# A transformer block on one Trainium2 core: one token tile loaded ahead of half a weight matrix, and two weight loads issued sooner

## The chip, the cores and the metric

The kernel runs on one core of one Trainium2 chip. The metric is the device time of one execution in microseconds (us). A set of runs is quoted by its median. The core has five engines, named as the profile names them: PE (TensorE, the matrix engine; PEld is its weight load), DVE (VectorE), ACT (ScalarE), POOL (GpSimd) and SP (SyncE). SP only issues transfers here; "SPq" is its queue.

## The reference

The reference is one block with linear attention and a gated feed-forward network (FFN), on 2048 tokens of width 1024, in bfloat16. Cut to what matters:

```python
def _A_ref(x, wqkv, wo):                      # B, S, D = 1, 2048, 1024
    H = 32; Dh = D // H
    q, k, v = ...(x @ wqkv)...                # three heads-first tensors
    phi = lambda t: jnp.where(t > 0, t + 1, jnp.exp(t)) + 1e-6
    pq, pk = phi(q), phi(k)
    kv = jnp.einsum("bhsd,bhse->bhde", pk, v)
    z = jnp.einsum("bhsd->bhd", pk)
    num = jnp.einsum("bhqd,bhde->bhqe", pq, kv)
    den = jnp.einsum("bhqd,bhd->bhq", pq, z)[..., None] + 1e-6
    return (num / den) ... @ wo

h = x + _A_ref(_layernorm(x), A_wqkv, A_wo)
h2 = h + _B_ref(_layernorm(h), W_gate, W_up, W_down)   # ((relu(gate) * up) @ W_down), F = 3584
```

## The kernel before

The tokens are cut into 16 tiles of 128. Large matrix products are done with a scheme of sums and differences of blocks that saves one block product in eight and costs DVE work: `w_sums` makes four differences of weight blocks for K (`twk`), V (`twv`) and Q (`twq`), and `x_sums` makes four sums of token blocks. Two places matter.

**The first place, the start.** Four buffers hold the incoming token tiles (`NX1 = 4`), so tile 6, the seventh, goes into the buffer of tile 2, and its load is issued by `ln1_norm(2)`, right after DVE has normalized tile 2. `load_wkv(0)` loads the first 512 columns of the K weights in two halves of 512 KB. All these calls only append to the program of each engine, in the order of the calls, so the order of the lines is the order in SP's queue and in DVE's work.

```python
def load_wkv(nt, half=None, eng="sp"):
    for hf in ([0, 1] if half is None else [half]):
        ...
        dma(sl_wkv[nt][hf], wkv[:, d0:d1, nt * NW:(nt + 1) * NW], ..., eng=eng)

def ln1_norm(st):
    ...                                   # DVE: (x - mean) * rstd
    if st in (2, 3):
        load_x1(st + NX1)                 # SP: tile 6 after tile 2, tile 7 after tile 3
```

```python
        ln1_norm(1)
        T1d(1)                            # SP: transposes of tile 1
        load_wkv(0)                       # SP: first and second half of the first K weights
        ...
        v_piece(0, 0, {5: lambda: T1c(1, 0), 7: lambda: T1c(1, 1)})
        ln1_norm(2)                       # DVE, then SP: load of tile 6
        v_piece(1, 0)
        ...
        ln1_norm(3)
        twk.pop(0)()                      # DVE: K weight difference
        ...
        ln1_stats(4)
        m5, q5 = ln1_stats_act(5)         # ACT: mean and square of tile 5
        v_piece(2, 1, {4: lambda: T1(3), 6: m5})
        q5()
        x_sums(0)
        twk.pop(0)()                      # DVE: K difference, reads the first half
        ln1_norm(4)
        T1d(4)
        m6, q6a, q6b = ln1_stats_act(6, True)
        v_piece(3, 0)
        m6()                              # ACT: mean of tile 6
        twk.pop(0)()
        ln1_norm(5)
        T1d(5)
        twk.pop(0)()                      # DVE: K difference, reads the second half
        twv.pop(0)()                      # DVE: two V differences, inputs there long before
        twv.pop(0)()
        v_piece(3, 1)
```

**The second place, the attention output products.** Step `t` of the loop does the numerators of tile `t` and the output product of an earlier tile on PE. SP's queue carries, in each step, the transposes that feed these products, a store, and in four of the steps a load of FFN weights (512 KB).

```python
        for t in range(NE, NST + LAG + 1):          # NE = 4
            if LAG <= t < NST + LAG:
                a4_mm(t - LAG)                      # PE: output product
            if t < NST:
                a2_num(t)                           # PE: numerators
                a2_div(t)                           # DVE: division; SP: transpose
            if LAG <= t < NST + LAG:
                a4_h(t - LAG)                       # DVE: residual; SP: store
                run(late_phi, 1)
            if LAG + 1 <= t < TPP + LAG + 1:
                a4_norm(t - LAG - 1)                # DVE: layer norm; SP: transpose
            if t in (5, 7, 18, 19):
                load_w_next()                       # SP: gate weights of the FFN
```

Of the kernel before, what the change touches and what calls it, by code (L numbers as in the profile page):

```python
# [132 lines left out]
def bass_sequential_preLN__linear_attn_block__glu_gated_reglu__prompt_kernel(  # L133
# [71 lines left out]
    with es:  # L205
# [148 lines left out]
        def bank(b, w=512):  # L354
            return ps[:, b, 0:w]
# [184 lines left out]
        def alloc_bank(pool, copied=False):  # L540

            b = min((b for b in pool if not (copied and b in partial)), key=lambda b: bank_last[b])
            if not copied:
                partial.discard(b)
            touch_bank(b)
            return b
# [19 lines left out]
        def dma(slot, dst_ap, src_ap, name, reads=(), writes=(), eng="sp"):  # L566
            return PL.add(eng, lambda e: e.dma_start(dst_ap, src_ap), reads=reads, writes=writes, slot=slot,  # L567
                          name=name)
# [5 lines left out]
        def load_x1(st, split=False):  # L574
            i = st % NX1
            if split:
                for c in range(NBC):
                    dma(sl_x1h[c], x1[:, i, c * BCH:(c + 1) * BCH], xv[st * P:(st + 1) * P, c * BCH:(c + 1) * BCH],
                        "ld_x1_%d_%d" % (st, c), writes=[B_x1[i][c]], eng=("sp", "act")[c])
            else:  # L580
                dma(sl_x1[i], x1[:, i, :], xv[st * P:(st + 1) * P, :], "ld_x1_%d" % st, writes=B_x1[i])
# [3 lines left out]
        def load_wkv(nt, half=None, eng="sp"):  # L585
            for hf in ([0, 1] if half is None else [half]):
                d0 = hf * WKH
                d1 = d0 + WKH
                dma(sl_wkv[nt][hf], wkv[:, d0:d1, nt * NW:(nt + 1) * NW],
                    wqkv_v[:, d0:d1, D + nt * NW:D + (nt + 1) * NW], "ld_wkv_%d_%d" % (nt, hf),  # L590
                    writes=[B_wkv[nt][hf]], eng=eng)
# [15 lines left out]
        def load_w_next():  # L607
            L = w_next[0]
            if L >= NPASS * NPAIR * 2:
                return  # L610
            w_next[0] += 1
            n_ = (L // 2) % NPAIR
            q, which = n_ - n_ % 2 + L % 2, n_ % 2
            i = L % NWG
            src = (wg_v if which == 0 else wu_v)[:, :, q * 2 * P:(q + 1) * 2 * P]
            dma(sl_w[i], wring[:, i, :, :], src, "ld_w_%d" % L, writes=[B_w[i]])
# [149 lines left out]
        def mm(out_ap, lhsT, rhs, start, stop, reads, bbuf, name, skip=False):  # L766
            return PL.add(
                "pe",
                lambda e: e.matmul(out_ap, lhsT, rhs, start=start, stop=stop, skip_group_check=skip),  # L769
                reads=reads, writes=[bbuf], name=name,  # L770
            )
# [66 lines left out]
        def ln_norm_dve(k, src_full, src_bufs, dst_ap, dst_buf, name):  # L838
            PL.add("dve", lambda e: e.tensor_scalar(out=dst_ap, in0=src_full, scalar1=mv[:, k, 0:1],
                                                    scalar2=rstd[:, k, :], op0=ALU.subtract, op1=ALU.mult),  # L840
                   reads=list(src_bufs) + [B_mv[k], B_rstd[k]], writes=[dst_buf], name=name + "_norm")
# [27 lines left out]
        def run(ops, n):  # L869
            for _ in range(min(n, len(ops))):  # L870
                ops.pop(0)()
# [19 lines left out]
        def ln1_norm(st):  # L891
            i = st % NX1
            if st in ln1_a:
                k = ln1_a[st]
                PL.add("dve", lambda e: e.tensor_scalar(out=xn[:, st % NXN, :], in0=x1[:, i, :], scalar1=s1[:, k, 0:1],
                                                        scalar2=s1[:, k, 2:3], op0=ALU.subtract, op1=ALU.mult),
                       reads=B_x1[i] + [B_s1[k][0], B_s1[k][2]], writes=[B_xn[st % NXN]], name="ln1_%d_norm" % st)
            else:
                ln_norm_dve(ln1_k.pop(st), x1[:, i, :], B_x1[i], xn[:, st % NXN, :], B_xn[st % NXN], "ln1_%d" % st)
            if st in (2, 3):  # L900
                load_x1(st + NX1)
# [24 lines left out]
        def T1c(st, hf):  # L926
            b = alloc_bank(P1_POOL)
            tb = bank_bf(b)
            for i in range(HDC):
                c = (hf * HDC + i) * P  # L930
                PL.add("pe", lambda e, i=i, c=c: e.transpose(tb[:, i, :], xn[:, 2 + st, c:c + P], ident[:]),
                       reads=[B_xc[st][hf], B_ident], writes=[B_bank[b]], name="T1c_%d" % st)
            PL.add("act", lambda e: e.activation(out=xcT[:, st, hf * HDC:(hf + 1) * HDC, :], in_=tb[:, 0:HDC, :],
                                                 func=ACTF.Identity),
                   reads=[B_bank[b]], writes=[B_xcT[st][hf]], name="evT1c_%d_%d" % (st, hf))
            partial.add(b)

        def T1d(st):
            k = st % NXN
            dma_t(sl_tx[k], xnT[:, :, st * P:(st + 1) * P], xn[:, k, :], "T1d_%d" % st, reads=[B_xn[k]],  # L940
                  writes=B_xnT[st])
            if st + NX1 < NST:
                load_x1(st + NX1)

        def xnT_buf(st, dc):
            return B_xnT[st][0 if dc < HDC else 1]
# [6 lines left out]
        def v_piece(st, h, mid=()):  # L953
            b = alloc_bank(P1_POOL)
            nt = ND2 + h
            mid = dict(mid)
            for dc in range(NDC):
                if dc in mid:
                    mid[dc]()
                if st < 2:  # L960
                    xa, bx = xcT[:, st, dc, :], B_xcT[st][dc // HDC]
                else:
                    xa, bx = xnT[:, dc, st * P:(st + 1) * P], xnT_buf(st, dc)
                mm(bank(b, NW), xa, wkv[:, dc, nt * NW:(nt + 1) * NW],
                   dc == 0, dc == NDC - 1, [bx, B_wkv[nt][0 if dc < WKH else 1]], B_bank[b],
                   "v_%d_%d" % (st, h))
            v_copy(b, st, h)
# [10 lines left out]
        def v_copy(b, st, j):  # L978
            sc, rd = (1.0, []) if st >= 2 else (rstd[:, v_k[st], :], [B_rstd[v_k[st]]])
            PL.add("act", lambda e: e.activation(out=v_out(st, j), in_=gw(bank(b)), func=ACTF.Identity, scale=sc),  # L980
                   reads=[B_bank[b]] + rd, writes=[B_v[st % NV][j]], name="v_%d_%d" % (st, j))
# [237 lines left out]
        def a2_num(st):  # L1219
            r, i, t = st // (NST // 2), (st % (NST // 2)) // 2, st % 2  # L1220
            for b_ in NB:
                touch_bank(b_)
            for g in range(NG):
                for h in range(HPG):
                    sl = slice(h * Dh, (h + 1) * Dh)
                    mm(ps[:, NB[h], g * NUW:g * NUW + Dh + 1], pqT[sl, r, t, g, i * P:(i + 1) * P],
                       kvz[sl, g, 0:Dh + 1], True, True, [B_pqT[r][t][g], B_kvz], B_bank[NB[h]],
                       "num_%d_%d" % (st, g), skip=True)
# [23 lines left out]
        def a4_mm(st):  # L1252
            k = st % NOT
            b = a4_bank[st] = min(H_PAIRS, key=lambda b: max(bank_last[b], bank_last[b + 1]))
            for nt in range(ND2):
                touch_bank(b + nt)
                for ct in range(NG):
                    mm(bank(b + nt, NW), oT[:, k, ct, :], wo[:, ct, nt * NW:(nt + 1) * NW],
                       ct == 0, ct == NG - 1, [B_oT[k], B_wo[nt]], B_bank[b + nt], "a4_%d_%d" % (st, nt))
# [704 lines left out]
            f_()  # L1964
        ln1_norm(1)
        T1d(1)
        load_wkv(0)
        for f_ in s2_[2:]:
            f_()
        twk = w_sums(wkv, bw_k, tw_k, B_TWk, "TWk", KH)  # L1970
# [2 lines left out]

        v_piece(0, 0, {5: lambda: T1c(1, 0), 7: lambda: T1c(1, 1)})
        ln1_norm(2)
        v_piece(1, 0)
        for f_ in s3:
            f_()
# [142 lines left out]
        for t in range(NE, NST + LAG + 1):  # L2121
            if LAG <= t < NST + LAG:
                a4_mm(t - LAG)
            if t < NST:
                a2_num(t)
                a2_div(t)
            if LAG <= t < NST + LAG:
                a4_h(t - LAG)
                run(late_phi, 1)
            if LAG + 1 <= t < TPP + LAG + 1:  # L2130
                a4_norm(t - LAG - 1)
            if t in (5, 7, 18, 19):
                load_w_next()
            if t >= 9:
                run(pool_t, 1)
            if 15 <= t < 19:
                s_sums()[t - 15]()
# [161 lines left out]
```

## Time and profile before

| | |
|---|---|
| three runs before the prediction | 722.75, 722.9 and 746.3 us, median 722.9 |
| the profiled execution | 723.54 us (span of the instructions 721.8 us) |
| PE's clock | 1.00 of full speed |
| PE busy | 710.7 us, 98% of the span |
| DVE busy, ACT busy | 589.0 and 358.9 us |

The run of 746.3 us is 3% above the other two. It is left out of every ratio; the median of this row still counts it (the two fast runs alone have 722.83). The second row matters later: the execution that was profiled took 0.64 us more than the median from which the prediction subtracts, and this could be seen when the prediction was made.

A line of a timeline reads: start in us, duration in us, engine, source line, operation, output and input, number of instructions. The part in square brackets is how long the engine was idle just before, and what the profile thinks ended the idling. Matmuls that follow each other are printed as one line. The bars of successive PE lines overlap a little, because matmuls are pipelined and their ends are modelled.

### The profile page before, as it was taken

How to read it: one execution, taken by the hardware profiler on the slowest of the kernel's cores; microseconds unless marked ns; L12 is line 12 of the kernel's file. 1: busy time of each engine (PE TensorE's matmuls, PEld its weight loads, DVE VectorE, ACT ScalarE, POOL GpSimd, SP SyncE). 2: the span in 40 equal slices, each digit the busy share in tenths (PEclk: the TensorE clock that was granted, in tenths of full speed). 3: DMA queues.
4: the chain of work that ended last, by engine and by line, in shares of the span. 5: the costliest groups of instructions: out<-in, count | busy, mean ns of one | idle time of the engine just before them, and what ended most of it. 6: DMA issues, size and time to landing. Idle time of an engine off the chain costs nothing.

```text
span 721.8 us, 12822 instructions
## 1 busy us (share of the span) xinstructions
PE 710.7 (98%) x4846; PEld 380.0 (53%) x4901; DVE 589.0 (82%) x1030; ACT 358.9 (50%) x626; POOL 111.4 (15%) x178
## 2 busy tenths in 40 slices
PE   8999999999999999999999999999999999999998
PEld 3344444444444444444444558865555555547887
DVE  6988867799776889889988787787889877888885
ACT  4877666764841456687756101035454445423010
POOL 3421100000360103322321002310000000000331
PEclk9999999999999999999999999999999999999999
DMA  9752244013998787999999989994555573037996
GB/s 294 260 107 71 38 128 161 12 30 67 203 231 257 237 272 238 270 314 306 294 279 268 313 251 322 311 217 116 155 159 147 156 244 90 1 92 248 323 319 186
DMA packets 195101, 144.17 MB, mean 200 GB/s; under 512 B 53984, under 2 KB 172512, under 8 KB 195040
## 3 DMA queue, kind: packets, MB, share of 16 engines
q1 hardware_dynamic: 190048, 138.77, 65.5%
q0 software_dynamic: 4032, 3.67, 3.6%
q10 hardware_dynamic: 960, 0.92, 0.4%
q8 instruction: 38, 0.62, 0.3%
q14 instruction: 23, 0.19, 0.1%
HBM read 98.76 MB, written 32.51 MB: 182 GB/s over the span
## 4 chain that ended last, share of the span: by engine, by line
PE 93%; DMA 2%; DVE 2%; issue 1%; ACT 1%; SPq 1%; ACTq 0%
PE ps L769 93%; DMA RE<-in_A_x_dram 2%; SPq L567 1%; ACT RXH L809 0%; DVE RWG L1016 0%; DVE RE L857 0%; DVE RX L1100 0%; ACT ps L774 0%; DVE RE L1674 0%; DVE RX L854 0%; DVE st L783 0%; DVE RW L991 0%; SPq L571 0%; ACT RX L850 0%; DVE RWG L1614 0%
## 5 line engine op out<-in xcount | busy, mean ns | idle before, releaser
L774 ACT ACTIVATE ps<-ps 128x512 f32<-128x512 f32 (+1 forms) x193 | 108.9, 565 | 221.7 <-PE ps L769 213.0
L769 PE MATMUL ps<-RC,RO 128*128 128x512 f16 x616 | 143.0, 369 | 0.0
L769 PE MATMUL ps<-RH,RWG 128*128 128x512 bf16 x447 | 107.9, 379 | 0.1
L769 PEld LDWEIGHTS ps<-RC,RO 128*128 128x128 f16 x616 | 60.3, 98 | 63.5
L769 PE MATMUL ps<-RC,RWG 128*128 128x512 f16 x320 | 76.9, 380 | 1.6 <-ACT ps L774 1.4
L769 PEld LDWEIGHTS ps<-RH,RWG 128*128 128x128 bf16 x448 | 43.8, 98 | 46.9
L1483 DVE TENSOR_TENSOR RAB<-ps,RAB 128x512 bf16<-128x512 f32 x56 | 37.3, 686 | 31.3 <-PE ps L769 31.3
L1683 POOL DMA_DIRECT2D out_dram<-RX x20 | 17.9, 1278 | 263.7 <-DVE RX L1674 221.5
L769 PE MATMUL ps<-RW,RE 128*128 128x512 bf16 x243 | 56.5, 379 | 1.5 <-DVE dtmp L1236 0.5
L769 PE MATMUL ps<-RH,RO 128*128 128x512 bf16 (+1 forms) x228 | 55.2, 379 | 1.5
L769 PE MATMUL ps<-RW,RAB 128*128 128x256 f16 (+3 forms) x358 | 52.5, 300 | 0.2
L769 PEld LDWEIGHTS ps<-RC,RWG 128*128 128x128 bf16 (+1 forms) x320 | 30.0, 98 | 41.5 <-ACT ps L774 7.5
L774 ACT ACTIVATE RE<-ps 128x512 f32<-128x512 f32 (+1 forms) x64 | 31.5, 503 | 37.8 <-PE ps L769 37.8
L769 PE MATMUL ps<-RAB 128*128 128x512 bf16 (+2 forms) x237 | 49.7, 348 | 0.1
L769 PEld LDWEIGHTS ps<-RW,RAB 128*128 128x128 f16 (+1 forms) x362 | 35.4, 98 | 14.4
L1674 DVE TENSOR_TENSOR RE<-ps,RE 128x512 f32<-128x512 f32 x44 | 30.2, 686 | 14.2 <-PE ps L769 13.7
L774 ACT ACTIVATE RAB<-ps 128x512 bf16<-128x512 f32 x56 | 33.3, 594 | 16.8 <-PE ps L769 16.4
L1367 DVE TENSOR_TENSOR RO<-RWG 128x1024 f16<-128x1024 bf16 x54 | 36.9, 683 | 4.5 <-DMA RWG<-in_B_W_up_dram 4.5
L769 PEld LDWEIGHTS ps<-RH,RO 128*128 128x128 f16 (+1 forms) x256 | 24.4, 98 | 29.9 <-ACT RX L774 1.5
L1478 ACT ACTIVATE RAB<-RAB 128x1024 bf16<-128x1024 bf16 x28 | 29.5, 1055 | 19.3 <-DVE RAB L1469 18.7
L769 PEld LDWEIGHTS ps<-RW,RE 128*128 128x128 bf16 x256 | 24.0, 98 | 28.7 <-DVE dtmp L1236 0.6
L1469 DVE TENSOR_TENSOR RAB<-ps,RE 128x512 bf16<-128x512 f32 x56 | 37.1, 685 | 2.2 <-PE ps L769 1.9
(170 smaller groups left out, 1169.1 us busy)
## 6 DMA issues: line engine op xcount, KB each, us to landing
RWG<-in_B_W_gate_dram SPq DMA_DIRECT2D x28, 512.0 KB, 6.3
RWG<-in_B_W_up_dram SPq DMA_DIRECT2D x28, 512.0 KB, 5.2
RW<-l_scr SPq DMA_DIRECT2D x20, 448.0 KB, 5.7
RW<-in_B_W_down_dram SPq DMA_DIRECT2D x14, 512.0 KB, 5.4
t_scr<-RW SPq DMA_DIRECT2D x14, 512.0 KB, 4.9
l_scr<-RX SPq DMA_DIRECT2D x7, 1024.0 KB, 5.9
RE<-l_scr SPq DMA_DIRECT2D x15, 448.0 KB, 4.8
RE<-in_A_x_dram SPq DMA_DIRECT2D x23, 256.0 KB, 3.6
```

The costliest lines, as they stand in the source:

```text
L567: return PL.add(eng, lambda e: e.dma_start(dst_ap, src_ap), reads=reads, writes=writes, slot=slot, name=name)
L769: lambda e: e.matmul(out_ap, lhsT, rhs, start=start, stop=stop, skip_group_check=skip),
L774: PL.add("act", lambda e: e.activation(out=dst, in_=src, func=func), reads=reads, writes=writes, name=name)
L1367: PL.add(eng, lambda e: e.tensor_tensor(out=tb(j, u), in0=f0(u), in1=f1(u), op=ALU.subtract), reads=[B_w[i + x] for x in r] + ([B_T[k + x] ...
L1469: PL.add("dve", lambda e: e.tensor_tensor(out=d, in0=src, in1=ftmp[:, u, :], op=ALU.add), reads=[bsrc, B_s5[u]], writes=[db], name=name)
L1478: PL.add("act", lambda e: e.activation(out=d, in_=d, func=ACTF.Relu), reads=[], writes=db, name=name)
L1483: PL.add("dve", lambda e: e.tensor_tensor(out=d, in0=bank(b), in1=d, op=ALU.mult), reads=[B_bank[b]], writes=[db], name=name)
L1674: PL.add(eng, lambda e: e.tensor_tensor(out=dst, in0=in0, in1=in1, op=op), reads=reads, writes=writes, name=name)
L1683: PL.add("pool", lambda e: e.dma_start(dst, src, accum_op=ALU.add), reads=[bsrc], writes=[B_hscr[st]], slot=sl, name="acc_%d_%d" % (st, dh))
```

## The change

The intent is to remove two idle spots of PE. In the start, tile 6 waits behind 1 MB of weights, so its load is put between the two halves. In the output products, a weight load stands in SP's queue right before a transpose that PE soon needs, so both loads are issued sooner.

```diff
         ln1_norm(1)
         T1d(1)
-        load_wkv(0)
+        load_wkv(0, half=0)
         for f_ in s2_[2:]:
             f_()
 ...
         v_piece(0, 0, {5: lambda: T1c(1, 0), 7: lambda: T1c(1, 1)})
         ln1_norm(2)
+        load_wkv(0, half=1)
         v_piece(1, 0)
 ...
-            if t in (5, 7, 18, 19):
+            if t in (4, 5, 18, 19):
                 load_w_next()
```

Below, "part 1" is the load order of the start and "part 2" is the earlier gate loads.

## The prediction

> **What bounds the kernel now.** I read the page's busy shares and its chain that ended last, then the chain in order of time, then the timelines of single engines around the two places that the diff touches. Busy shares and chain shares:
>
> ```profile
> PE 710.7 (98%) x4846; PEld 380.0 (53%) x4901; DVE 589.0 (82%) x1030; ACT 358.9 (50%) x626; POOL 111.4 (15%) x178
> ...
> PE 93%; DMA 2%; DVE 2%; issue 1%; ACT 1%; SPq 1%; ACTq 0%
> ```
>
> TensorE (PE) is busy 710.7 of 721.8 us. A change that takes no matmul away can win only PE's idle time, 11.1 us in the whole kernel, so nothing near 2% (14.5 us) can come of it. The question is how much of the idle time belongs to the two places. First place, the chain in order of time (start, duration, what):
>
> ```profile
> 15.80 0.43 SPq L567
> 16.27 0.51 SPq L567
> 16.89 6.53 DMA RE<-in_A_x_dram
> 23.50 1.15 ACT RXH L809 x2
> ```
>
> The first two lines are SyncE's queue issuing the two halves of the first K weights (512 KB each); the third is the load of token tile 6, the seventh (256 KB), queued behind both and landing 6.53 us later, at 23.42; the fourth is ScalarE (ACT) taking that tile's mean, which had waited. ACT, then PE, then VectorE (DVE), from their timelines (start, duration, instruction, idle before):
>
> ```profile
> 21.77 0.61 ACT L980 ACTIVATE RE<-ps 128x512 bf16<-128x512 f32 x1
> 23.50 1.06 ACT L809 ACTIVATE RXH<-RE 128x1024 bf16<-128x1024 bf16 x1 [1.12 <-DMA RE<-in_A_x_dram]
> 24.46 0.19 ACT L809 ACTIVATION_READ_ACCUMULATOR RXH<-RE 128x1 f32 x1
> 24.55 0.58 ACT L980 ACTIVATE RE<-ps 128x512 bf16<-128x512 f32 x1
> 25.03 0.59 ACT L774 ACTIVATE ps<-ps 128x512 f32<-128x512 f32 x1
> ```
> ```profile
> 23.23 1.03 PE L769 MATMUL ps<-RC,RWG 128*128 128x512 f16 x4
> 25.67 1.04 PE L769 MATMUL ps<-RC,RWG 128*128 128x512 f16 x4 [1.42 <-ACT ps L774]
> ```
> ```profile
> 26.70 1.23 DVE L991 TENSOR_TENSOR RW<-RAB,RW 128x2048 f16<-128x2048 bf16 x1
> 28.47 0.29 DVE L854 TENSOR_SCALAR RX<-RX 128x512 bf16<-128x512 bf16 x1 [0.55 <-ACT RX L850]
> 28.80 0.69 DVE L857 SCALAR_TENSOR_TENSOR RE<-ps,RX 128x512 bf16<-128x512 f32 x1
> ```
>
> ACT loses 1.12 us for the tile. Everything it does next comes late, and one of those (25.03, a copy between PSUM banks) is what PE's next product waits for: 1.42 us idle. Later DVE idles 0.55 us for an ACT exponential. From 28.47 to past 38 DVE has no marked wait: there it, and not ACT, sets the pace, and the chain runs through it up to 36.25, where PE takes over. Second place, the attention output products, SyncE and then PE:
>
> ```profile
> 183.58 0.58 SPq L567 DMA_DIRECT2D RWG<-in_B_W_gate_dram  x1
> ...
> 193.20 0.58 SPq L567 DMA_DIRECT2D RWG<-in_B_W_gate_dram  x1
> 193.89 2.54 SPq L571 DMA_TRANSPOSE RE<-RE  x1
> ...
> 198.50 1.24 SPq L571 DMA_TRANSPOSE RE<-RE  x1
> ```
> ```profile
> 198.31 0.37 PE L769 MATMUL ps<-kvz,RAB 32*128 32x33 bf16 x32
> 199.17 3.61 PE L769 MATMUL ps<-RW,RE 128*128 128x512 bf16 x16 [0.49 <-DVE dtmp L1236]
> 202.71 0.37 PE L769 MATMUL ps<-kvz,RAB 32*128 32x33 bf16 x32
> 203.44 3.40 PE L769 MATMUL ps<-RW,RE 128*128 128x512 bf16 x15 [0.35 <-DMA RE<-RE]
> ```
>
> SyncE's single queue carries the transposes that feed these products, the stores and these loads. The transpose issued at 193.89 lands 5.1 us later, at about 199.0; the one at 198.50 lands 4.6 us later, at 203.1. PE starts the products on those tiles at 199.17 and 203.44, after 0.49 and 0.35 us of idling. The first wait is put down to DVE, but that product does not read what DVE wrote; the landing at 199.0 fits it. The inputs had long been ready: DVE finished the tile moved at 193.89 at 189.2, and the one moved at 198.50 at 193.05. So the queue itself is late here.
>
> **What the Trainium skill says.** "Perfetto Trace Analysis", section "DMA Instruction — HWDGE (DVE, Sync)": the bar of such an instruction covers the taking of the descriptor generator and the generation, not the movement. The trace agrees: bars of about 0.5 us, landing 4.7 to 6.5 us after the start for the loads around 16 us; and the same kind of transpose has a bar of 1.24 us at 198.50 but 2.54 us directly behind a 512 KB load, so I count the longer bar as queueing. "DMA: Bandwidth & Descriptors", section "Queues, rings and completion order": each DMA engine takes the descriptors of one ring in ring order, though completion is not strictly first in, first out. The landings fit: tile 5 at 18.98, first half 20.5, second half 22.8, tile 6 23.4. "TensorE: Matmul & The Clock Gate", section "Back-to-back issue gap", gives about 216 ns for an isolated gap at 512 columns; here four such matmuls advance PE 0.86 to 0.87 us (26.55, 27.41, 28.27), 215 ns each, at clock 1.00. That is the pace from which I measure lost time.
>
> **Part 1, tile 6 ahead of the second half.** Nothing is added or removed; two transfers swap. Tile 6 must wait for DVE's normalization of tile 2 to release its buffer, but that ends at 11.9 us (11.36 + 0.55) and SyncE comes to it only at 16.27, so it blocks nothing. DMA moved 338 GB/s from 16 to 22 us: skipping 512 KB saves 524,288 B / 338 GB/s = 1.55 us, so the tile lands near 21.9 instead of 23.42. ACT is free at 22.38 (21.77 + 0.61): the whole wait of 1.12 us goes, with some 0.5 us to spare. The second half slips by 256 KB / 338 GB/s = 0.8 us, from 22.8 to some 23.6. Its first reader is DVE's fourth weight difference at 24.31, itself behind a DVE instruction held by POOL since 23.40; PE reads it at 26.55, or 25.45 in the new order. So it stays hidden.
>
> ACT's copy moves from 25.03 to 23.95, PE's product from 25.67 to 24.55. But this does not carry through. ACT's exponential comes 1.1 us earlier, while DVE is busy with weight differences until about 27.9 whatever ACT does. DVE gains its idle 0.55 us and no more, and from there it sets the pace until PE starts its run at 36.79. PE gives 0.55 us back at the product at 32.12, whose copy in ACT's order stands behind an exponential that waits for DVE. Both transposes of tiles 4 and 5, which DVE reads at 29.41, are issued by 24.42 and not moved; tile 4's landed in 2.7 us and by the same time tile 5's is there near 27.1. **Part 1 is worth 0.55 us.**
>
> **Part 2, gate loads two steps sooner.** The first load goes from step 5 to step 4, the second from step 7 to step 5. Step 4's place in the queue follows the store at 175.07; SyncE is idle from 175.65 to 177.66, so it is issued there for free and lands about 4.8 us later, at 180.5. The transpose at 177.66 may stretch to 2.5 us, but its product is not due before 187.0. The second load takes the place of the first, at 183.58, unchanged. At 193.20 none is left: 0.62 to 0.69 us of issue go, and the next transpose's bar should fall from 2.54 to 1.24 us, so 2.0 us in all. It lands near 193.25 + 3.1 = 196.4 instead of 199.0, and the following one, issued near 196.5 instead of 198.5, near 200. PE wants them at 198.68 and 202.5: both waits vanish. Steps without a wait are 3.865 us apart (171.25 to 198.31, seven steps); 198.31 to 206.77 took 8.46 for two. **Part 2 is worth 8.46 - 7.73 = 0.73 us**, as PE is the chain before and after. POOL's weight differences, which read the second load, run from 197.9 on in their turn behind the normalization, and lie beside PE; the later loads hang on the last output tiles and move with PE.
>
> **Sum.** 722.9 - 0.55 - 0.73 = 721.6 us, 0.18% less.
>
> **The rivals.** First, the whole 1.12 us of part 1 carries through, if DVE can be earlier after all: 721.0 us. For it: PE's largest single gap is right there. Against: DVE's weight differences stand back to back from 24.31 to 27.9. Second, the tile does not come in time, because its landing follows the slowest of the DMA engines: DMA had fallen to 86 GB/s from 22.5 to 23.0 us and to 29 in the next half, before tile 6 was reported landed. A late second half could also hold DVE at 24.31. Part 1 is then worth 0 to 0.3 us: 721.9 to 722.2. Third, in part 2 SyncE falls behind at another place: two loads in steps 4 and 5 press on the first stores and transposes and PE waits for an earlier tile, or contention elsewhere eats the gain: 722.3 to 723. Against: the transpose issued at 188.79 landed in 4.5 us, at 193.3, and was wanted at 194.75; that slack of 1.4 us is not touched, as the load ahead of it is issued at the same time as before. Fourth, the whole gain shrinks because the shift moves later transfers against each other: a few tenths either way.
>
> **Range and chances.** Both parts right gives 721.6; both rivals for the better 721.0, less 0.2 for luck; both failing 722.7. So 720.8 to 722.7 for 8 in 10. PE's idle total rules out 2% faster; 2% slower would need a new stall of 14 us or a measurement in the slow execution that one of the three runs before shows (746.3).
>
> **What would show it.** Part 1: ACT's mark of 1.12 us for the tile is gone, PE's gap before the product now at 25.67 falls from 1.42 to about 0.3 us, DVE's 0.55 us is gone, and PE's product at 37.44 starts near 36.9. Part 2: gate loads near 175.1 and 183.0 us, none near 193; no PE idle in the output products; the first FFN matmuls (228.70) start near 227.4. It is wrong if 37.44 has not moved (part 1 hidden), has moved by over 0.9 us (DVE was not the limit), if an output product waits for a transpose still, or if the 1.3 us present at 228 us are gone by the end.

## The result

| | runs in us | median |
|---|---|---|
| before, the three of above and one more | 722.75, 722.9, 723.78 (and 746.3, slow) | 723.34 |
| after | 722.08, 722.08, 722.1, 722.21 | 722.09 |

A ratio in this document is the mean time of one kernel's fast runs over the mean of the other's fast runs of the same rounds, so it is not quite the ratio of the medians quoted. Here it is 0.9986, with a 95% interval from 0.9966 to 1.0005: the same within 2%, as predicted. The 722.09 us lie in the range, 0.5 us above the point. The difference of the two medians, 1.25 us, is too large, because 723.34 counts the slow run: the three fast runs alone have a median of 722.9, and 722.09 is 0.81 us below it. The profiled execution of the changed kernel took 722.21 us.

The profile's summary page of the changed kernel, busy times and the shares of the chain that ended last:

```profile
PE 714.3 (99%) x4901; PEld 380.0 (53%) x4901; DVE 588.9 (82%) x1030; ACT 358.9 (50%) x626; POOL 110.8 (15%) x178
...
PE 95%; DVE 2%; DMA 1%; ACT 1%; issue 1%; SPq 0%; ACTq 0%
```

The loads' share of the chain has fallen from 2% to 1%, because the wait for tile 6 is out of it. The rise of PE's busy time from 710.7 to 714.3 us is no effect of the change: the count of matmuls has risen from 4846 to 4901, so 55 records were missing in the trace before. Sums of busy time are therefore no measure of gain here; start times of instructions are.

The start, ACT and then PE and then DVE of the changed kernel:

```profile
21.86 0.61 ACT L980 ACTIVATE RE<-ps 128x512 bf16<-128x512 f32 x1
22.35 1.06 ACT L809 ACTIVATE RXH<-RE 128x1024 bf16<-128x1024 bf16 x1
...
23.89 0.59 ACT L774 ACTIVATE ps<-ps 128x512 f32<-128x512 f32 x1
```
```profile
23.31 1.03 PE L769 MATMUL ps<-RC,RWG 128*128 128x512 f16 x4
24.54 1.04 PE L769 MATMUL ps<-RC,RWG 128*128 128x512 f16 x4 [0.20 <-ACT ps L774]
...
31.56 1.04 PE L769 MATMUL ps<-RW,RWG 128*128 128x512 f16 x4 [0.81 <-ACT ps L774]
...
36.88 1.03 PE L769 MATMUL ps<-RAB 128*128 128x512 bf16 x4
```
```profile
26.78 1.22 DVE L991 TENSOR_TENSOR RW<-RAB,RW 128x2048 f16<-128x2048 bf16 x1
27.92 0.28 DVE L854 TENSOR_SCALAR RX<-RX 128x512 bf16<-128x512 bf16 x1
```

ACT takes the mean of tile 6 at 22.35 without a mark of a wait (waits under 0.15 us are not marked). PE's gap has shrunk from 1.42 to 0.20 us, DVE's idle 0.55 us is gone, PE gives some of it back at 31.56 (0.81 us), and the product that began at 37.44 begins at 36.88. Each of these is what the prediction named.

The output products, SP's queue and then PE:

```profile
175.09 0.44 SPq L567 DMA_DIRECT2D RWG<-in_B_W_gate_dram  x1
...
182.98 0.59 SPq L567 DMA_DIRECT2D RWG<-in_B_W_gate_dram  x1
...
192.26 1.24 SPq L571 DMA_TRANSPOSE RE<-RE  x1
...
195.57 1.24 SPq L571 DMA_TRANSPOSE RE<-RE  x1
```
```profile
198.00 3.63 PE L769 MATMUL ps<-RW,RE 128*128 128x512 bf16 x16
...
201.87 3.63 PE L769 MATMUL ps<-RW,RE 128*128 128x512 bf16 x16
...
227.36 1.89 PE L769 MATMUL ps<-RH,RWG 128*128 128x512 bf16 x8
```

Both loads are where the prediction put them, no product waits, and the FFN begins at 227.36 (predicted 227.4). Read from this pair of traces alone, the prediction is right in every line. The experiments show that this pair was a lucky one.

### The profile page after: what moved, and what is told of

It reads as the page before. It is cut to its first block, busy times and chain, and to the rows that moved or that the text cites. A ratio compares the mean times of both kernels' runs of the same rounds, so it can differ in the third digit from the quotient of the medians.

```text
span 720.5 us, 12877 instructions
## 1 busy us (share of the span) xinstructions
PE 714.3 (99%) x4901; PEld 380.0 (53%) x4901; DVE 588.9 (82%) x1030; ACT 358.9 (50%) x626; POOL 110.8 (15%) x178
## 4 chain that ended last, share of the span: by engine, by line
PE 95%; DVE 2%; DMA 1%; ACT 1%; issue 1%; SPq 0%; ACTq 0%
PE ps L769 95%; DMA RAB<-in_A_wqkv_dram 1%; DVE RWG L1016 0%; DVE RE L857 0%; DVE RX L1100 0%; DVE RE L1674 0%; DVE RX L854 0%; DVE RH L1016 0%; ACT RXH L809 0%; DVE RC L991 0%; DVE RW L991 0%; ACT ps L774 0%; PE ps L910 0%; DVE RWG L1614 0%; SPq L567 0%
## 5 line engine op out<-in xcount | busy, mean ns | idle before, releaser
L769 PE MATMUL ps<-RH,RO 128*128 128x512 bf16 (+1 forms) x256 | 61.2, 379 | 0.0
L1367 DVE TENSOR_TENSOR RO<-RWG 128x1024 f16<-128x1024 bf16 x54 | 36.9, 684 | 4.5 <-DMA RWG<-in_B_W_up_dram 4.5
```

Source lines behind the costliest of these rows:

```text
L769: lambda e: e.matmul(out_ap, lhsT, rhs, start=start, stop=stop, skip_group_check=skip),
L1367: PL.add(eng, lambda e: e.tensor_tensor(out=tb(j, u), in0=f0(u), in1=f1(u), op=ALU.subtract), reads=[B_w[i + x] for x in r] + ([B_T[k + x] ...
```

## A measure finer than the clock

Executions of one kernel differ by more than the effect: in one set, 11 runs of the kernel before went from 722.47 to 724.91 us. The upper end has a mark: wherever a run's clock is listed, the eleven executions with a mean granted clock of 0.998 took 724.27 us or more. The only one of them that was traced (part 2 alone, below) stood 2.34 us for the very first weights, and its granted clock was 0.57 from 8 to 12 us. No edit here touches that. So the timed ratios below, with intervals of about 0.13% (0.9 us) to each side, cannot tell half a microsecond. The traces can, because starts are given to 0.01 us and the work between two fixed instructions is the same in all kernels. I use three instructions of PE, which the prediction already named: A is the product before the large gap of the start (23.23 in the trace before), B is the first product of the second group (37.44), C is the first matmul of the FFN (228.70). B and C in the trace before:

```profile
37.44 1.03 PE L769 MATMUL ps<-RAB 128*128 128x512 bf16 x4
...
228.70 1.89 PE L769 MATMUL ps<-RH,RWG 128*128 128x512 bf16 x8
```

B - A then holds what part 1 does, and C - B what part 2 does. From C to the end of the span it is 493.1 us to within 0.1 us in all traces, so nothing is given back later.

| kernel (trace) | first half of K weights lands after | A | B | C | span | B - A | C - B |
|---|---|---|---|---|---|---|---|
| before | 4.7 us | 23.23 | 37.44 | 228.70 | 721.8 | 14.21 | 191.26 |
| before, second trace | 4.1 | 22.89 | 37.19 | 227.68 | 720.8 | 14.30 | 190.49 |
| first gate load alone moved | 5.7 | 23.13 | 37.54 | 228.04 | 721.2 | 14.41 | 190.50 |
| second gate load on ACT's queue | 4.1 | 23.19 | 37.52 | 228.02 | 721.1 | 14.33 | 190.50 |
| both gate loads at step 5 | 5.7 | 23.10 | 37.40 | 230.32 | 723.4 | 14.30 | 192.92 |
| part 2 alone | 4.2 | 26.26 | 39.24 | 229.73 | 722.8 | 12.98 | 190.49 |
| before, DVE reordered | 5.9 | 23.16 | 37.56 | 228.05 | 721.2 | 14.40 | 190.49 |
| after | 4.3 | 23.31 | 36.88 | 227.36 | 720.5 | 13.57 | 190.48 |
| after, second trace | 5.8 | 23.38 | 37.36 | 227.85 | 720.9 | 13.98 | 190.49 |
| part 1 alone | 6.1 | 23.36 | 37.41 | 228.19 | 721.3 | 14.05 | 190.78 |
| after, half a difference on POOL | 4.3 | 23.50 | 37.35 | 227.85 | 721.0 | 13.85 | 190.50 |
| after, DVE reordered | 5.8 | 23.09 | 36.38 | 226.87 | 720.0 | 13.29 | 190.49 |
| part 1, DVE reordered | 5.4 | 23.33 | 37.18 | 227.72 | 720.8 | 13.85 | 190.54 |

The second column is the time from the start of the issue of the first half of the K weights to its landing. The kernel before sends exactly the same issue at this place as the kernels with part 1.

## The experiments

Ten further kernels, and the two kernels of above once more, make twelve runs in four sets; each set has its own runs of the kernel before on the same chip, and the sets ran on different chips. All gave correct outputs.

### First set: the parts alone, and the queue (median of before: 723.39 us, nine runs)

**Part 1 alone.** The theory was the prediction's: 0.55 us from part 1 and 0.73 us from part 2, independent. The edit is the first two hunks of the change, with the steps left at `(5, 7, 18, 19)`.

> Tile 6 ahead of the second half of the K weights, gate loads left at steps 5 and 7. My theory (DVE paces the chain from 28 us on): PE's idle time before the product near 24.5 us falls from 1.42 to about 0.2 us, but the product near 31.6 us idles about 0.8 us instead of 0.23, so the product at 37.44 us starts near 36.9; the waits for transposes near 199 and 203 us stay (0.49 and 0.35 us); time 0.55 us less than before. Rival (the two parts depend on each other, or the 0.55 us is lost again before the end): 0 to 0.2 us less.

Measured: 723.04 us (five runs, 722.41 to 725.08), ratio 0.9999, interval 0.9987 to 1.0012. In the trace the tile was in time, but B came at 37.41 and not at 36.9. DVE, first difference that reads the first half and later the instruction that had idled 0.55 us, and then PE:

```profile
21.73 1.23 DVE L991 TENSOR_TENSOR RC<-RAB 128x2048 f16<-128x2048 bf16 x1 [1.34 <-DMA RAB<-in_A_wqkv_dram]
...
28.45 0.29 DVE L854 TENSOR_SCALAR RX<-RX 128x512 bf16<-128x512 bf16 x1
```
```profile
32.09 1.04 PE L769 MATMUL ps<-RW,RWG 128*128 128x512 f16 x4 [1.19 <-ACT ps L774]
```

DVE stood 1.34 us for the first half of the K weights, which landed 6.1 us after its issue. Its later work shifts with it: the instruction at 28.45 no longer waits for ACT, but it starts as late as in the kernel before (28.47). PE gives back 1.19 us at 32.09 instead of 0.81. The expected waits of the transposes were also wrong: 0.15 us in all (the product at 202.71 is 4.02 us behind the one at 198.69, instead of 3.865), where the same measure gave 0.73 us in the trace before. So the part that the load order wins depends on a transfer that the change does not touch, and the second place does not always lose time with the old steps.

**Part 2 alone.** The edit is the last hunk of the change only.

> Gate loads at steps 4 and 5, start of the kernel as before. My theory: the start has the 1.42 us of PE idle time still and the product at 37.44 us does not move, no output product waits, the first FFN matmul starts near 227.97 instead of 228.70 us; time 0.73 us less than before. Rival (the queue would not have been late in the shifted kernel, or part 1 helped part 2): some of the wait for transposes stays, 0.3 us less or fewer.

Measured: 723.09 us (722.82 to 724.58), ratio 0.9996, interval 0.9983 to 1.001. No output product waits, and C - B is 190.49. The start of this one execution says nothing: PE stood for the very first weights.

```profile
8.74 2.31 PE L769 MATMUL ps<-RAB,RC 128*128 128x512 bf16 x5 [2.34 <-DMA RAB<-in_A_wqkv_dram]
```

With everything after it 2 to 3 us later, tile 6 was no longer late, and B - A is 12.98. I leave this row out of what follows on part 1.

**First gate load alone moved.** The edit:

```diff
-            if t in (5, 7, 18, 19):
+            if t in (4, 7, 18, 19):
```

> Only the first gate load moves, from step 5 to step 4; the second stays at step 7. My theory (it is the second load, directly ahead of the transpose that feeds the late product, that makes SyncE late): the waits near 199 and 203 us stay at about 0.5 and 0.3 us, time as before within 0.2 us. Rival (what counts is the total that has queued up on SyncE by then, so that the first load's place is worth as much): both waits shrink by half or more, 0.4 us less or better.

Measured: 722.96 us (722.7 to 724.68), ratio 1.0003, interval 0.999 to 1.0015. The expectation was wrong: the second load still stands in the old place (192.75), and no product waits (C - B 190.50). Either the first load was the cause, or the waits of the trace before were chance. The run has a second use. DVE in its timeline:

```profile
21.48 1.23 DVE L991 TENSOR_TENSOR RC<-RAB 128x2048 f16<-128x2048 bf16 x1 [0.92 <-DMA RAB<-in_A_wqkv_dram]
...
28.58 0.29 DVE L854 TENSOR_SCALAR RX<-RX 128x512 bf16<-128x512 bf16 x1 [0.30 <-ACT RX L850]
```

Here, in the old load order, the first half is late too (5.7 us) and DVE stands 0.92 us for it. But DVE then still waits 0.30 us for ACT, which is late because of tile 6. Two late arrivals lie side by side, and B - A is 14.41, hardly more than the 14.21 to 14.33 of traces in which the first half came early.

**Both gate loads at step 5.** This overdoes the third rival, pressure of two loads on the queue. The edit:

```diff
-            if t in (5, 7, 18, 19):
+            if t == 5:
+                load_w_next()
+                load_w_next()
+            if t in (18, 19):
                 load_w_next()
```

> Both gate loads at step 5, one behind the other; nothing at steps 4 and 7. My theory: the waits near 199 and 203 us go as in the full change, but 1 MB stands ahead of the transposes of steps 6 and 7, and the one of step 7, which had 1.4 us to spare, comes about 1.5 to 2 us later; so a new wait of 0 to 0.6 us near 194.8 us, net 0.2 to 0.7 us less than before. Rival (the first load's move to step 4 does nothing): no wait anywhere in the output products, 0.73 us less, as with steps 4 and 5.

Measured: 725.18 us (724.4 to 726.79), ratio 1.003, interval 1.0016 to 1.0043, so really longer. SP and PE:

```profile
183.51 1.21 SPq L567 DMA_DIRECT2D RWG<-in_B_W_gate_dram  x2
185.24 2.66 SPq L571 DMA_TRANSPOSE RE<-RE  x1
```
```profile
193.25 3.61 PE L769 MATMUL ps<-RW,RE 128*128 128x512 bf16 x16 [2.38 <-DMA RE<-RE]
```

The transpose directly behind the two loads (1 MB) landed 7.9 us after its start, at 193.1, where PE wanted it at 190.87. I had named a later transpose and expected 0 to 0.6 us. So loads ahead of a transpose do delay it and PE does stand for it: the mechanism behind part 2 is real. It is a question of how much slack there is in a given execution.

### Second set: is DVE now the limit, and is the queue itself the cause? (median of before: 723.1 us, eleven runs)

**Half of one weight difference on POOL, in the kernel before and in the changed one.** If DVE sets the pace after part 1, less DVE work should help after and not before. The edit to each:

```diff
+        def twv1(eng, d0, d1):
+            PL.add(eng, lambda e: e.tensor_tensor(out=TWv[:, 0, d0:d1, :], in0=wv_[:, d0:d1, NW:2 * NW],
+                                                  in1=wv_[:, d0:d1, 0:NW], op=ALU.subtract), ...)
+        twv1("pool", 0, KH // 2)
+        twv[1] = lambda: twv1("dve", KH // 2, KH)
```

> Kernel before, with half of one DVE weight difference (the second V one, 1.22 us on DVE near 25.4 us) done by POOL near 16 us: DVE's work before its exponential falls by about 0.6 us. My theory: in the kernel before ACT is late for the tile and DVE waits for it, so DVE's idle time before 28.47 us grows from 0.55 to about 1.15 us and PE's product at 37.44 us does not move; time as before within 0.2 us. Rival (DVE's work is the limit there already): 37.44 moves 0.3 to 0.6 us earlier and the time with it.

> Changed kernel with the same half of a weight difference on POOL. My theory (with the tile early, DVE is what keeps half of the won 1.12 us): DVE starts its phi work near 27.4 instead of 27.92 us, PE's idle time before the product at 31.56 us falls from 0.81 to about 0.3 us, PE's product at 36.88 starts near 36.4; 0.4 to 0.6 us less than the changed kernel, 1.7 to 1.9 less than before. Rival (PE, or the order of ACT's work, is the limit): 36.88 does not move. A third outcome: POOL's 2.3 us delay its own normalization steps and DVE waits for them; then DVE's idle time before 23.93 us grows from 0.46 us and the gain is partly lost.

Neither told the theories apart. In the kernel before, the profiled execution took 2861.66 us. PE alone was slow: it was busy 2855.8 us, while DVE was busy 603.0 us against 589.0, and yet the page shows the clock at 1.0. Its start can't be compared with the others. The other four runs were 722.71 to 722.84 (ratio 0.9992). In the changed kernel a third thing came: 722.81 us (722.65 to 722.97), ratio 0.9993, interval 0.9981 to 1.0004. POOL's new instruction and the DVE normalization that runs beside it:

```profile
15.41 2.11 POOL L1981 TENSOR_TENSOR RW<-RAB 128x1024 f16<-128x1024 bf16 x1
```
```profile
15.54 2.26 DVE L839 TENSOR_SCALAR RXH<-RE,mv,rstd 128x1024 bf16<-128x1024 bf16 x1 [0.51 <-POOL rstd L795]
```

The normalization took 2.26 us instead of 0.55 us, about until POOL was done. The Trainium skill, "SBUF — State Buffer", section "Who interferes with whom", says that DVE in certain modes and POOL need the same pair of ports, that whoever issues first gets it for its whole instruction, and that the other is fully blocked; it counts a DVE instruction of this kind among those that can. This run agrees as far as it can show: the normalization ended at 17.80, and POOL at 17.52 (ends on POOL are rough). DVE lost 1.7 us here and saved about half of a difference of 1.22 us later, so that its instruction of 27.92 began at 28.36.

**Second gate load on ACT's queue.** Step 7's load is issued by ACT instead of SP, so that SP's queue is free for the transpose.

```diff
-        def load_w_next():
+        def load_w_next(eng="sp"):
 ...
-            dma(sl_w[i], wring[:, i, :, :], src, "ld_w_%d" % L, writes=[B_w[i]])
+            dma(sl_w[i], wring[:, i, :, :], src, "ld_w_%d" % L, writes=[B_w[i]], eng=eng)
 ...
-                load_w_next()
+                load_w_next("act" if t == 7 else "sp")
```

> Kernel before, second gate load still at step 7 but issued by ACT's queue. It separates SyncE's time from the bytes. If it is SyncE's issue time and the descriptors ahead in its own ring: the transpose now at 193.89 us starts near 193.2 with a bar of about 1.24 us and both waits go, 0.7 us less than before. If it is the 512 KB on the shared DMA engines, whoever issues them: the bar stays near 2.5 us, the transpose lands about 0.6 us earlier only, and of the 0.49 and 0.35 us at least a part stays; 0.2 to 0.7 us less. The load itself costs ACT about 0.5 us, which it has to spare there.

Measured: 723.38 us (722.88 to 725.09, six runs), ratio 1.0005, interval 0.9992 to 1.0018. The output products hardly waited (C - B 190.50). It would speak for the queue, but the edit changed more than the queue: ACT issued the load at 187.94, some 5 us before SP did in the trace before (193.20). And the next run, where the unchanged kernel does not wait either, takes the rest away.

### Third set: both kernels again, and DVE's order (median of before: 722.87 us, nine runs)

**The kernel before, unchanged, as a run of its own.**

> The kernel before, unchanged, for a second trace of it: the seven experiments so far show the landing of the first half of the K weights anywhere from 4.1 to 6.1 us after its issue, and no wait for transposes near 199 and 203 us in three of the kernels that should have had it. If the profile of before was typical: the 1.12 us wait of ACT for tile 6 and both waits for transposes (0.49 and 0.35 us) are there again within 0.2 us. If the waits for transposes come from run-to-run spread of SyncE's bars: the tile wait is there, but the sum of the transpose waits is anywhere from 0 to 0.8 us. Time as before by construction; it shows the noise.

Measured: 722.54 us (722.51 to 723.14), ratio 0.9999, interval 0.9985 to 1.0012; its median is 0.33 us under that of the same kernel's other runs of the set, which shows what a difference of medians is worth here. ACT, then PE in the start:

```profile
23.25 1.06 ACT L809 ACTIVATE RXH<-RE 128x1024 bf16<-128x1024 bf16 x1 [1.21 <-DMA RE<-in_A_x_dram]
```
```profile
25.43 1.04 PE L769 MATMUL ps<-RC,RWG 128*128 128x512 f16 x4 [1.51 <-ACT ps L774]
...
37.19 1.03 PE L769 MATMUL ps<-RAB 128*128 128x512 bf16 x4
```

The wait for tile 6 is there again, so part 1 works on something that the kernel before always has. The output products, SP and PE:

```profile
192.21 0.59 SPq L567 DMA_DIRECT2D RWG<-in_B_W_gate_dram  x1
192.91 1.79 SPq L571 DMA_TRANSPOSE RE<-RE  x1
```
```profile
198.32 3.63 PE L769 MATMUL ps<-RW,RE 128*128 128x512 bf16 x16
...
202.41 3.40 PE L769 MATMUL ps<-RW,RE 128*128 128x512 bf16 x15 [0.16 <-issue]
...
227.68 1.89 PE L769 MATMUL ps<-RH,RWG 128*128 128x512 bf16 x8
```

The load stands before the transpose as it did, but the transpose has a bar of 1.79 us instead of 2.54 and landed 4.9 us after its start, at 197.8, before PE wanted it at 198.32. The product at 202.41 shows 15 matmuls instead of 16 and "issue" before it: that is a missing record and no wait, as C - B is 190.49. So the two waits of 0.49 and 0.35 us, from which the prediction worked out part 2, are not in every execution of this kernel.

**The changed kernel again.**

> The changed kernel again, for a second trace and a time beside before on the same chip. If both parts are worth what I predicted in every run: 1.2 to 1.3 us less than before. If part 1 is only worth its 0.55 us when the first half of the K weights lands early, and part 2 its 0.73 us only when SyncE is late: 0.4 to 1.0 us less on average; and in the trace the product at 36.88 us lies between 36.9 and 37.5 according to that landing (36.9 if it takes under 4.8 us from issue, 37.4 if about 6).

Measured: 722.53 us (722.68, 722.68, 721.9, 722.53, 721.83), ratio 0.9992, interval 0.998 to 1.0005. The traced one has the late first half (5.8 us), DVE idle 0.93 us for it, B at 37.36 as the second expectation said, B - A 13.98, and no wait in the output products. The timed runs look like two groups 0.8 us apart; early and late first halves would make some 0.4 us of that, and I can't show the rest.

**DVE's order changed, in the changed kernel and in the kernel before.** The theory by now: with part 1, DVE sets the pace, and a late first half costs time. Then DVE should do first what it has inputs for. A V difference, whose inputs have been there for long, goes before the K differences that need the late halves:

```diff
         x_sums(0)
-        twk.pop(0)()
         ln1_norm(4)
         T1d(4)
+        twv.pop(0)()
         m6, q6a, q6b = ln1_stats_act(6, True)
         v_piece(3, 0)
         m6()
         twk.pop(0)()
+        twk.pop(0)()
         ln1_norm(5)
         T1d(5)
         twk.pop(0)()
         twv.pop(0)()
-        twv.pop(0)()
```

> Changed kernel with DVE's work between 20.3 and 28 us in another order, none added or taken away: tile 4's normalization and the second V weight difference, whose inputs are there early, come first, then the K differences, so DVE neither waits for the first half of the K weights nor for POOL's value for tile 5 (0.46 us). Theory (DVE is the limit once the tile is early): DVE's first phi step starts near 27.4 instead of 27.92 us, PE idles about 0.3 instead of 0.81 us near 31 us, the product at 36.88 starts near 36.4; 0.4 to 0.6 us less than the changed kernel when the first half lands early, about 1 us less when late, and less spread. Rival (ACT or PE sets the pace): 36.88 does not move, or PE now waits for a K difference near 24.5 us.

> Kernel before with the same new order of DVE's work. Theory (in the kernel before ACT is late for tile 6, and DVE only waits for it): DVE's idle time before its first phi step grows from 0.55 to about 1.0 us, the product at 37.44 us does not move by over 0.15 us; time as before within 0.3 us. Rival (DVE sets the pace in both): 37.44 moves 0.4 us or more earlier.

The changed kernel with this order: 721.92 us (721.61, 721.72, 721.92, 722.15 and one of 724.27), ratio 0.9992, interval 0.998 to 1.0005. The kernel before with it: 722.64 us (722.55 to 722.88), ratio 0.9997, interval 0.9984 to 1.0009. DVE and PE of the reordered changed kernel, and then DVE of the reordered kernel before:

```profile
26.30 1.22 DVE L991 TENSOR_TENSOR RW<-RAB,RW 128x2048 f16<-128x2048 bf16 x1
27.43 0.28 DVE L854 TENSOR_SCALAR RX<-RX 128x512 bf16<-128x512 bf16 x1
```
```profile
31.07 1.04 PE L769 MATMUL ps<-RW,RWG 128*128 128x512 f16 x4 [0.47 <-ACT ps L774]
...
36.38 1.03 PE L769 MATMUL ps<-RAB 128*128 128x512 bf16 x4
```
```profile
26.48 1.22 DVE L991 TENSOR_TENSOR RW<-RAB,RW 128x2048 f16<-128x2048 bf16 x1
28.60 0.29 DVE L854 TENSOR_SCALAR RX<-RX 128x512 bf16<-128x512 bf16 x1 [0.91 <-ACT RX L850]
```

This pair tells the theories apart. In both, DVE is done with the differences about as early (27.5 and 27.7). In the changed kernel it goes straight on at 27.43 and B - A falls to 13.29, the lowest of all traces with a usual start, though the first half was late (5.8 us). In the kernel before it stands 0.91 us for ACT, and B - A is 14.40, no gain at all. So before, ACT limits this stretch because tile 6 is late; after, DVE limits it.

### Fourth set: what is left without part 2 (median of before: 723.34 us, nine runs)

**Part 1 with DVE reordered, old steps of the gate loads.** If part 2 seldom matters, this should do as well as the full change reordered. The edit is that of part 1 and of the reordering together.

> Part 1 with the new order of DVE's work, gate loads left at steps 5 and 7. Theory (part 2 was worth only what that one profiled execution of the kernel before had lost in waits for transposes, and a second trace of before had none of them; DVE's order is what makes part 1 pay whatever the landing of the first half): 0.7 to 1.0 us less than before, as the reordered kernel with both parts; the product at 36.88 us starts near 36.4; the waits for transposes near 198 and 202 us sum to under 0.3 us. Rival (part 2 is worth its 0.73 us in most executions): 0.3 us less than before or no gain, and the two waits are in the trace with some 0.7 us together.

Measured: 722.19 us (722.08 to 722.56), ratio 0.9982, interval 0.9968 to 0.9995. The median is 1.15 us below that of before. It is the only faster kernel whose interval leaves out 1; with twelve runs tried, one such interval is weak evidence by itself, and the traces carry the argument. The profiled execution was the longest of the five, and B came at 37.18 and not at 36.4. ACT in its timeline:

```profile
20.00 1.06 ACT L809 ACTIVATE RXH<-RE 128x1024 bf16<-128x1024 bf16 x1 [0.57 <-DVE RWG L1016]
```

This is the mean of tile 5. The profile names a DVE instruction as the releaser, but what this instruction reads is tile 5, which landed 4.6 us after an issue at 15.29, at 19.93; the landing fits and DVE does not. So a further load of the start can be the late one. The waits in the output products are 0.05 us in all (C - B 190.54), as expected.

## Why the prediction was right or wrong

**What held.** No matmul was removed, PE's idle time bounds the gain, and the time moved by a few tenths of a percent at most: 722.09 us was inside the range. The bound itself, 11.1 us of idle time, was too high: the line that it was read from has 4846 matmuls beside 4901 weight loads, and the missing 55 count there as idle. In the complete record of the changed kernel the idle time is 720.5 - 714.3 = 6.2 us. Part 1's mechanism is as told. The tile's wait was in every trace of the old order with a usual start (1.12 to 1.32 us), and it is marked in no trace with part 1. Most of the 1.12 us does not carry through because DVE sets the pace next; the reordered pair shows this, since DVE's order changes B - A with part 1 (13.29) and not without it (14.40). The first rival, the full 1.12 us, and the claim that gains are lost at the end both fall: C to the end is 493.1 us in every trace.

**"Part 1 is worth 0.55 us" is a term mis-sized.** The five traces of the old load order and old DVE order with a usual start have a mean B - A of 14.31 us. With part 1 it is 13.57, 13.98 and 14.05, so it is worth 0.74, 0.33 or 0.26 us, by single traces from different chips. The large one had the first half of the K weights after 4.3 us, the others after 5.8 and 6.1 us. The prediction took the landing of one trace (4.7 us) as fixed and looked only at the second half for a rival. It missed that the first half has the same effect one instruction earlier on DVE: before, its lateness is hidden beside ACT's, and after, nothing hides it.

**"With some 0.5 us to spare" was too much.** Tile 6 landed 5.9 us after an issue at 16.38, at 22.27, where 21.9 had been worked out from the mean rate. ACT began at 22.35, 0.08 us after the landing. Where it had stood waiting, in the trace before, it also began 0.08 us after the landing (23.42 and 23.50). So nothing was left to spare; in the second trace and in part 1 alone the two times are again 0.08 us apart (22.35 and 22.43, 22.39 and 22.47). The second rival had warned of a late landing; it did not come to pass by a hair.

**"Part 2 is worth 8.46 - 7.73 = 0.73 us" is the step that failed.** The arithmetic was right for the execution that had been profiled: C - B was 191.26 there and is 190.48 after. But the prediction subtracted it from the median of 722.9 us, while that execution took 723.54. Its excess of 0.64 us is about the loss that was subtracted, so an execution that takes the median need not have had it to give. Six traces have the second gate load at step 7 in SP's queue (before, its second trace, before reordered, first load alone moved, part 1 alone, part 1 reordered). Over 190.49 us they lose 0.77, 0, 0, 0.01, 0.29 and 0.05 us. Of the 0.29 only 0.15 are at the transposes; the rest is at a product at 45.68 that waited for DVE, and is given to neither part here (counted against part 1, it would leave 0.12 us of that trace's 0.26). With 0.15 in its place the mean is 0.98 / 6 = 0.16 us. The five traces with the loads at steps 4 and 5 are all at 190.48 to 190.50. So part 2 takes away a loss that happens now and then, of 0.16 us on average by this small sample, and the run with both loads at step 5 shows the mechanism enlarged. How often the loss happens is not known: of the nine runs of the kernel before in the first set, seven took 723.36 to 723.83 us, much like the profiled one, and none of them was traced.

**Why the sum still fitted.** The trace after had an early first half (4.3 us) and was compared with a trace before that had lost time at the transposes. Worked again from the means: part 1 gives (0.74 + 0.33 + 0.26) / 3 = 0.44 us and part 2 some 0.16 us, together 0.6 us instead of 1.28. The two timed comparisons of the changed kernel gave medians 0.81 us (fast runs alone) and 0.34 us lower, both with intervals that include no change.

**What stays open.** Why the first half lands after 4.1 us in one execution and 6.1 us in another is not known. With the old order it was 4.7, 4.1, 5.7, 4.1, 5.7, 4.2 and 5.9 us, with part 1 it was 4.3, 5.8, 6.1, 4.3, 5.8 and 5.4 us; these are too few to say whether part 1 itself makes late landings likelier. Why the transposes behind the same load take longer in some executions is open as well.

## What to carry to other kernels

Before you subtract the waits of a profiled execution from a median, check that this execution took the median time, and take a second trace of the same kernel: a wait that is in only one of them is worth only its share. When an early transfer frees one engine, ask which engine sets the pace next and what that one waits for; let it do first the work whose inputs are already there. When the clock scatters more than the effect, compare the starts of fixed instructions in the traces, stretch by stretch.

## What the Trainium skill lacked or had wrong

- "TensorE: Matmul & The Clock Gate", section "Back-to-back issue gap": it gives about 131 ns a matmul for a stream of weight load and matmul at 512 columns, and about 216 ns only for an isolated one. Here every matmul has its own weight load (4901 of each) and four of them advance PE by 0.86 to 0.87 us, 215 ns each, in the stream.
- "DMA: Bandwidth & Descriptors": it gives latencies, but not how much the landing of one and the same issue varies from one execution to the next. Here the same 512 KB, issued at the same place, landed after 4.1 to 6.1 us in thirteen traces. It also has no figure for a transpose behind loads in the same queue: 7.9 us from start to landing behind 1 MB, against 4.9 us and 5.1 us behind 512 KB.
- "Perfetto Trace Analysis": it does not say to hold the profiled execution's own time against the usual one. Here 723.54 against 722.9 us was a hint that two of its waits (0.49 and 0.35 us) might not be usual; the second trace had neither.
- "TensorE: Matmul & The Clock Gate", section "Seeing it yourself": it warns of a clock stuck at a quarter for over 50 us and of clock events that can't be trusted. It has no case that lasts a whole execution: here 2861.66 us against some 722.8, with PE slow throughout and the clock shown at 1.0.
